# Linear attention into a gated FFN: the weight fold first, in column quarters over SyncE's queue, and the loads in a new order

## The chip, the cores and the metric

The kernel runs on one core of one Trainium2 chip. The metric is the device time of one execution in microseconds (us). A profiled execution gives the trace; its span runs from the first to the last instruction of the program.

## The reference

```python
def phi(x):
    return np.where(x > 0, x, np.exp(x) - 1.0) + 1.0
q_p, k_p = (phi(q), phi(k))                       # q, k, v: 8 batches, 8 heads, 576 tokens, 64
kv = np.einsum('bhsd,bhse->bhde', k_p, v)
z = np.sum(k_p, axis=2)
num = np.einsum('bhsd,bhde->bhse', q_p, kv)
den = np.einsum('bhsd,bhd->bhs', q_p, z)[..., None] + 1e-06
attn = num / den
...
x = attn.transpose(0, 2, 1, 3).reshape(4608, 512)
h = ((x @ w1) * (x @ w2)) @ w3                    # w1, w2: 512 x 1024; w3: 1024 x 1024
out = h @ w_out                                   # w_out: 1024 x 512
```

Inputs and output are f32 in HBM; the matmuls take bf16.

## The kernel before, in words

**The fold.** Since nothing stands between `@ w3` and `@ w_out`, the kernel multiplies the two weights once, `wf = w3 @ w_out`, and then needs one product per token block instead of two. For each of w3's eight row tiles (128 rows) `w3_tr` (L132) transposes eight 128x128 blocks on TensorE into a PSUM tile `w3p` and copies it to `w3t`; `wf_mm` (L139) then makes eight matmuls of 512 columns against `wo_sb` (w_out in bf16) and a copy into `wf_sb`.

**The work of a batch.** 512 of a batch's 576 tokens are handled per batch, as four blocks j of 128; the 64 that are left (the tail) are gathered over the batches into a ninth block, 8. For each batch, phi is made of k and q: an exp on ScalarE (`phi_exp`), a max and add on VectorE (`phi_max1`), a min on VectorE (`phi_min`), each for two halves g of four heads and for the tail. v is cast to bf16 (`v_unit`). `kv_full` multiplies k and v (L225, L229), `nat` (L262) multiplies q, transposed, with that (L280) and divides (L284 to L286) into `xn`. q is transposed either on TensorE (`q_tr`, L251, batches 0 and 1) or by a DMA (`qt_load`, L246); `xn` is transposed the same two ways (`xt_tr` L297, `xt_load` L304). The FFN of a block is eight F units (`f_unit`, L330: eight matmuls of 512 columns into `a_ps` and `b_ps`, a copy on ScalarE at L327, a product on VectorE at L328) and four O units (`o_unit` L475, eight matmuls of 512 columns each, and a copy), then stores (`o_store`); `o_last` (L497) does an O unit in two column halves, which are copied and stored by two engines.

**The order.** `ORDER` is a list written out in the program; each engine executes its own part of it in that order, and so does each DMA queue. A token is a letter, a batch and a part:

- loads: `M` q, `L` k, `N` v (512 KB a half), `R` the tails (part 0 four loads of 64 KB of q and k, part 1 two of v), `B` a column quarter of w1 (part 0) or w2 (part 1), `E` a w3 row tile, `C` w_out
- `x y z` exp, max and min of k, `X Y Z` of q, `v` the cast of v, `w` the transposes of a w3 tile, `u` a tile's fold matmuls
- `a` q's transposes on TensorE, `T` by DMA; `K` kv_full; `A` nat of block j; `P` xn's transposes on TensorE, `D` by DMA
- `F` and `O` the units (F0.7: unit 7 of block 0), `h` and `i` F0.0 and F0.1 step by step, `S H` stores, `Q` o_last, `I` constants

A "+" picks the other engine: for loads GpSimd's queue instead of SyncE's (SP), for copies VectorE instead of ScalarE.

**Queues.** The DMAs that SP issues and those that GpSimd issues each form one queue; both use the same 16 DMA engines. Only GpSimd's loads convert from f32 to bf16 on their way. So w3, w_out, w1 and w2 all go over GpSimd's queue and land as bf16. At the start SP issues half of q and k of batch 0 and its tails, and then nothing until the transposing DMAs at 45.6 us; all else of the front is GpSimd's, in the order q, w_out, w3, k, v, w3, k, w3, q of batch 1, k of batch 1, tails, w1 and w2 with v of batch 1 between them, tails. Each of the two queues has eight semaphores: a ninth load waits for the first one's landing. f32 loads of q, k and v go into the 13 buffers of the pool `ld`. `load_tail` (L99) issues four or two DMAs and returns the last.

**PSUM.** `mm_ps` has four banks (F units, fold), `o_ps_p` two (O units and transposes), `at_ps` one tile of two banks (kv_full and nat).

The functions for a Strassen scheme (`ws_make`, `xs_make`, `g_unit`, `s_make`, `w_unit`, `wt_make` and what they call) stand in the program, but the order has no token for them. `GATES` is empty.

## Time and profile before

| | us |
|---|---|
| median of 3 runs | 259.39 (259.12 to 259.40) |
| span of the profiled execution | 257.4 |
| around the span (median less span) | 2.0 |
| first matmul starts | 13.15 |
| first F unit starts | 40.70 |
| last matmul ends | 252.6 |
| TensorE busy | 232.3 (90%) |
| VectorE, ScalarE, GpSimd busy | 159.1, 116.8, 49.1 |
| HBM read, written | 38.80 MB, 9.44 MB |

The profiled execution is known by its span alone; what lies around it is taken from the runs' median. In the profile, PE is TensorE, PEld its weight loads, DVE VectorE, ACT ScalarE, POOL GpSimd and SP SyncE; L322 is line 322. Matmuls overlap, so a matmul's own duration (379 ns with 512 columns) is longer than its share of PE's time when matmuls follow each other (216 ns). A wait line names who waited, for whom, the total, how often, and the longest.

### The profile page before, as it was taken

The page shows a single profiled execution, that of the slowest core. Times are in us where ns is not written, and L with a number is a line of the kernel's source. Part 1 is how long each engine was busy: PE and PEld are TensorE (multiplying, and loading weights), DVE is VectorE, ACT ScalarE, POOL GpSimd, SP SyncE. Part 2 cuts the span into 40 slices and gives each one's busy share as a digit, 9 for nine tenths or more (in the row PEclk, how much of TensorE's full clock was granted, in tenths as well). Part 3 has the DMA queues.
Part 4 walks back from the last instruction along what each step waited for, and adds up shares of the span by engine and source line. Part 5 has one row for each costly group of instructions (what it writes and reads, how often), then busy time and mean ns, then how long its engine had stood idle before and what let it go on. Part 6 is the DMA issues. An engine that isn't in the chain of part 4 may idle for free.

```text
span 257.4 us, 3788 instructions
## 1 busy us (share of the span) xinstructions
PE 232.3 (90%) x1352; PEld 117.8 (46%) x1368; DVE 159.1 (62%) x350; ACT 116.8 (45%) x180; POOL 49.1 (19%) x84
## 2 busy tenths in 40 slices
PE   0087899999999869999999999999999999999992
PEld 0063565554454434445445445454544444444540
DVE  0548589778899426897887899978235633343200
ACT  1404677357756506755562473645332312332221
POOL 8524479455045100600000000000000000000000
PEclk9999999999999979999999999999999999999999
DMA  6999999999989999799999998646512143001124
GB/s 220 211 237 289 311 255 245 200 248 283 299 247 291 194 242 347 182 284 222 356 308 211 289 263 272 154 89 151 200 20 91 74 83 163 3 0 30 42 115 139
DMA packets 63762, 50.57 MB, mean 196 GB/s; under 512 B 33536, under 2 KB 58368, under 8 KB 63744
## 3 DMA queue, kind: packets, MB, share of 16 engines
q1 hardware_dynamic: 54432, 37.10, 55.9%
q0 software_dynamic: 9152, 13.11, 23.4%
q8 instruction: 10, 0.16, 0.3%
q10 hardware_dynamic: 160, 0.13, 0.2%
q14 instruction: 8, 0.07, 0.1%
HBM read 38.80 MB, written 9.44 MB: 187 GB/s over the span
## 4 chain that ended last, share of the span: by engine, by line
PE 78%; DMA 13%; DVE 4%; issue 2%; ACT 0%; POOL 0%; DVEq 0%; ACTq 0%; POOLq 0%
PE a_ps L322 24%; PE b_ps L322 23%; PE o_ps L479 21%; DMA v<-in_v_dram 5%; DMA qt<-qj 4%; PE nd L280 4%; DMA wt_sb<-in_moe_w_out_dram 4%; PE kvp L225 2%; PE wf_ps L143 1%; PE kvp L229 1%; DVE y L173 1%; DVE vt L204 1%; PE o_ps L504 1%; DVE kj L198 1%; DVE qj L198 0%
## 5 line engine op out<-in xcount | busy, mean ns | idle before, releaser
L322 PEld LDWEIGHTS <-w_sb 128*128 128x128 bf16 x576 | 55.3, 98 | 61.8 <-issue 0.9
L328 DVE TENSOR_TENSOR ab<-a_sb,b_ps 128x512 bf16<-128x512 f32 x72 | 49.1, 685 | 38.2 <-PE b_ps L322 30.5
L322 PE MATMUL a_ps<-xt,w_sb 128*128 128x512 bf16 x256 | 67.3, 382 | 0.0
L322 PE MATMUL b_ps<-xt,w_sb 128*128 128x512 bf16 x256 | 66.7, 379 | 0.0
L327 ACT COPY a_sb<-a_ps 128x512 f32<-128x512 f32 x72 | 41.8, 585 | 54.4 <-PE a_ps L322 48.9
L479 PE MATMUL o_ps<-wf_sb,ab 128*128 128x512 bf16 x267 | 63.7, 383 | 0.8 <-issue 0.2
L479 PEld LDWEIGHTS <-ab 128*128 128x128 bf16 x280 | 27.0, 98 | 30.2 <-issue 0.8
L481 ACT COPY o_sb<-o_ps 128x512 f32<-128x512 f32 x29 | 16.8, 585 | 43.4 <-PE o_ps L479 27.2
L286 DVE TENSOR_TENSOR xn<-nd,r 128x512 bf16<-128x512 f32 x32 | 22.1, 691 | 1.1
L168 ACT ACTIVATE e<-q 128x1024 bf16<-128x1024 f32 x16 | 16.7, 1056 | 8.5 <-DMA q<-in_q_dram 8.5
L168 ACT ACTIVATE e<-k 128x1024 bf16<-128x1024 f32 x16 | 16.6, 1056 | 5.2 <-DMA k<-in_k_dram 5.0
L280 PE MATMUL nd<-kv,qt 128*128 128x130 bf16 (+1 forms) x160 | 16.1, 223 | 2.6 <-DMA qt<-qj 2.1
L136 PE MATMUL w3p<-ident,w3b 128*128 128x128 bf16 x64 | 5.7, 242 | 13.7 <-DMA w3b<-in_moe_w_dram 13.7
L280 PEld LDWEIGHTS <-qt 128*128 128x128 bf16 (+1 forms) x160 | 11.6, 101 | 14.0 <-issue 3.3
L284 DVE TENSOR_SCALAR r<-nd 128x8 f32<-128x8 f32 (+1 forms) x40 | 6.5, 162 | 16.8 <-PE nd L280 16.4
L173 DVE TENSOR_SCALAR y<-q 128x1024 bf16<-128x1024 f32 x16 | 11.2, 707 | 8.7 <-DMA q<-in_q_dram 8.7
L143 PE MATMUL wf_ps<-wt_sb,w3t 128*128 128x512 bf16 x61 | 14.9, 380 | 0.7 <-DMA wt_sb<-in_moe_w_out_dram 0.5
L104 POOL DMA_DIRECT2D qk32r<-in_q_dram x14 | 9.0, 648 | 19.1 <-ACT a_sb L327 16.5
L198 DVE TENSOR_TENSOR qj<-e,y 128x512 bf16<-128x512 bf16 x32 | 11.9, 417 | 0.4 <-ACT e L168 0.3
L198 DVE TENSOR_TENSOR kj<-e,y 128x512 bf16<-128x512 bf16 x32 | 11.9, 418 | 0.2
L225 PE MATMUL kvp<-vt,kj 128*128 128x130 bf16 x128 | 9.8, 219 | 2.4 <-DVE vt L204 1.8
L136 PEld LDWEIGHTS <-w3b 128*128 128x128 bf16 x64 | 4.6, 109 | 15.0 <-DMA w3b<-in_moe_w_dram 14.5
(54 smaller groups left out, 180.3 us busy)
## 6 DMA issues: line engine op xcount, KB each, us to landing
out_dram<-o_sb SPq DMA_DIRECT2D x16, 512.0 KB, 3.7
q<-in_q_dram SPq DMA_DIRECT2D x13, 512.0 KB, 8.0
k<-in_k_dram SPq DMA_DIRECT2D x13, 512.0 KB, 6.7
v<-in_v_dram SPq DMA_DIRECT2D x12, 512.0 KB, 8.0
w3b<-in_moe_w_dram POOLq DMA_DIRECT2D x8, 256.0 KB, 12.0
v<-in_v_dram POOLq DMA_DIRECT2D x4, 512.0 KB, 9.8
w_sb<-in_moe_w_dram POOLq DMA_DIRECT2D x8, 256.0 KB, 6.9
q<-in_q_dram POOLq DMA_DIRECT2D x3, 512.0 KB, 11.2
```

The costliest lines, as they stand in the source:

```text
L143: nc.tensor.matmul(wfs[i], w3ts[i][:, kc, :], wo_sb[:, kc, :], start=(kc == 0), stop=(kc == FC - 1))
L168: nc.scalar.activation(out=e, in_=x, func=AF.Exp)
L173: (nc.gpsimd if alt else nc.vector).tensor_scalar(out=y, in0=x, scalar1=0.0, scalar2=1.0, op0=ALU.max, op1=ALU.add)
L198: nc.vector.tensor_tensor(out=p[0][:, 2 * g + c].rearrange("p j u d -> p u j d"), in0=e[:, c], in1=y[:, c], op=ALU.min)
L225: nc.tensor.matmul(kvp[:, i, g * W:(g + 1) * W], kj[:, hp, j].rearrange("p u d -> p (u d)"), vt[:, j, 2 * hp:2 * hp + 2, :].rearrange("p h ...
L280: nc.tensor.matmul(nd[rows, g, i * 2 * E1:(i + 1) * 2 * E1], w, kvs[b % 2][:, i, g].rearrange("p u e -> p (u e)"), start=True, stop=True)
L286: nc.vector.tensor_tensor(out=dst.rearrange("p (g h) e -> p g h e", g=2), in0=v4[:, :, :, 0:D], in1=r[rows].unsqueeze(3).to_broadcast([n, ...
L322: nc.tensor.matmul(ps, w[:, kc, f * P:(f + 1) * P], xt_of(c)[:, :, kc, :], start=(kc == 0), stop=(kc == KC - 1))
L327: nc.scalar.copy(out=a_sb, in_=a_ps)
L328: nc.vector.tensor_mul(out=abs_[c][:, f, :], in0=a_sb, in1=b_ps)
L479: nc.tensor.matmul(o_ps, ab[:, f, m * P:(m + 1) * P], wf_sb[:, f, :], start=(f == 0), stop=(f == FC - 1))
L481: copy_of(alt)(out=rows_of(c, m // 2)[:, m % 2], in_=o_ps)
```

## The change

- **The fold's first half comes first, by column quarters.** w3's row tiles 0 to 3 are loaded in four column quarters of 512 KB (`load_w3q`, token `c`; the first in two halves of 256 KB), w_out in four row quarters of 512 KB (`load_wo`, `C`), in turn, as f32 over SP's queue into the `ld` buffers. They are cast on chip: `w3_cast` (`g`, half a quarter each) and `wo_cast` (`G`). `q3_tr` (`W`) transposes a quarter's eight blocks, `q3_mm` (`U`) adds a quarter's two matmuls to a row tile's PSUM bank, so that four banks collect over the four quarters; `wf_copy` (`j`) is the copy. Row tiles 4 to 7 stay as they were (`E`, `w`, `u`), with the copy as a token of its own.
- **Loads.** All other loads of batches 0 to 2, w3's tiles 4 to 7, w1 and w2 go over GpSimd's queue, in one line: tails and k of batch 0, w3 and v in between, q, w3, then w1, w2 with k of batch 1, then v, tails and q of batch 1, then tails, k, v and q of batch 2. From batch 3 on all loads, tails too, go over SP's queue. Token `pC1` makes the next GpSimd load wait until w_out's second quarter is in; `qM1.1` makes the next SP load wait until q of batch 1 is in.
- **q of batch 0 by tokens.** Its halves are the blocks j 0, 1 and j 2, 3 of all heads, in runs of 512 B (`BY_TOKEN`), not four heads of all blocks in runs of 1 KB; `phi_min` and `q_tr` follow.
- **Tails of q in batches 0 and 1** are transposed on TensorE (two transposes, a0.2 and a1.2) instead of by DMA (T0.1, T1.1).
- **Twelve matmuls on zeros** (`zeros`, `d12`) at the start of TensorE's work.
- **Two F units of block 0 in token halves** (`f0.0.0` and so on), as the first two and the last two blocks j come; this takes the place of `h` and `i`.
- **nat** in batches 0 and 1 makes the last product in two halves; kvp and nd share one tile `at` that is allocated once.
- **The end.** Besides Q8.3, the last unit of all is an `o_last` (Q7.2), whose PSUM tile now comes from `mm_ps`.
- The order is a new one throughout. The Strassen functions and `GATES` go.

The diff's core:

```diff
+    def load_wo(qd):
+        t = raw["wo", qd] = ld.tile([P, HW], F32, tag="ld", name="wo32")
+        return nc.sync.dma_start(
+            out=t.rearrange("p (c n) -> p c n", n=DM),
+            in_=moe_w_out.rearrange("(c p) n -> p c n", p=P)[:, 2 * qd:2 * qd + 2, :])
+
+    def load_w3q(qd, h):
+        if ("w3q", qd) not in raw:
+            raw["w3q", qd] = ld.tile([P, HW], F32, tag="ld", name="w332")
+        ts = slice(2 * h, 2 * h + 2) if h < 2 else slice(0, 4)
+        return nc.sync.dma_start(
+            out=raw["w3q", qd].rearrange("p (t n) -> p t n", n=WQ)[:, ts],
+            in_=moe_w3.rearrange("(t p) n -> p t n", p=P)[:, ts, qd * WQ:(qd + 1) * WQ])
...
+    def w3_cast(qd, h, alt):
...
+        copy_of(alt)(out=raw["w3", 0][:, 2 * h:2 * h + 2, qd * WQ:(qd + 1) * WQ],
+                     in_=raw["w3q", qd].rearrange("p (t n) -> p t n", n=WQ)[:, 2 * h:2 * h + 2])
+
+    def wo_cast(qd, alt):
+        copy_of(alt)(out=wo_sb[:, 2 * qd:2 * qd + 2, :],
+                     in_=raw["wo", qd].rearrange("p (c n) -> p c n", n=DM))
+
+    def q3_tr(qd, alt):
+        t = w3ts["q", qd] = e_p.tile([P, 4, 2, P], BF16, tag="e", name="w3t", bufs=4)
+        tp = o_ps_p.tile([P, 4, 2, P], BF16, tag="ou"[qd % 2], name="w3p")
+        for i in range(4):
+            for c in range(2):
+                kc = 2 * qd + c
+                nc.tensor.transpose(tp[:, i, c, :], raw["w3", 0][:, i, kc * P:(kc + 1) * P], ident)
+        copy_of(alt)(out=t, in_=tp)
+
+    def q3_mm(qd, i):
+        if qd == 0:
+            wfs[i] = mm_ps.tile([P, DM], F32, tag="mm", name="wf_ps")
+        for c in range(2):
+            kc = 2 * qd + c
+            nc.tensor.matmul(wfs[i], w3ts["q", qd][:, i, c, :], wo_sb[:, kc, :],
+                             start=(kc == 0), stop=(kc == FC - 1))
...
+    def zeros(n):
+        for _ in range(n):
+            nc.tensor.matmul(at[:, 0], zero[:, 0:P], zero, start=True, stop=True)
...
+        js = slice(0, NJ) if half is None else slice(2 * half, 2 * half + 2)
+        for ps, w in ((a_ps, w1_sb), (b_ps, w2_sb)):
+            for kc in range(KC):
+                nc.tensor.matmul(ps[:, js.start * P:js.stop * P], w[:, kc, f * P:(f + 1) * P],
+                                 xt_of(c)[:, js, kc, :], start=(kc == 0 and half != 1),
+                                 stop=(kc == KC - 1), skip_group_check=half is not None)
...
-    M0.0+ Y0.0 C1 E0 M0.1 I0 X0.0 E3 X0.1 L0.0 Y0.1 Z0.0 Z0.1 C0 y0.0 w0+ R0.0 R0.1 x0.0 E4 x0.2
-    I1 w3+ L0.1+ x0.1 a0.0+ E1 y0.2 a0.1+ N0.1+ u0.2+ N0.0+ z0.0 R1.1 v0.1 y0.1 w4+ u3.2+ E2 w1+
...
+    I0 I3 c0.0 g0.0 d12 c0.1 g0.1+ I1+ C0 G0+ W0+ c1.2 g1.0 g1.1+ U0.3 W1 U0.2 U0.1 U0.0 C1 c2.2 G1
+    U1.1 U1.0 C2 g2.0 g2.1 U1.3 W2 U1.2 c3.2 g3.1+ G2 g3.0 W3 U2.0 C3 U2.3 pC1 R0.0+ R0.1+ G3+ y0.2
+    U2.2 U2.1 U3.0 L0.0+ U3.2 x0.2 x0.0 j2 E4 v0.2+ w4 U3.1 U3.3 y0.0 j0+ z0.2 u4.0 L0.1+ I2 y0.1
+    N0.0+ E5 u4.1 N0.1+ j3 x0.1 E6 M0.0+ M0.1+ j1 j4 a0.2 w5+ z0.0 u5.0 v0.0+ z0.1 E7 v0.1 u5.1 w6+
+    X0.0 B0.0 K0 Y0.0 Z0.0 Y0.1 u6.0 a0.0+ X0.1 w7 Z0.1 B0.1 A0.1 u6.1 a0.1 A0.0 u7.0 B1.0 B1.1 u7.1
+    P0.1 L1.0+ A0.3 j5 j7 P0.0+ A0.2 P0.3+ B2.0 B2.1 f0.0.0 A0.4 y1.0 j6 B3.0 B3.1 L1.1+ N1.0+ x1.0
+    P0.2 f0.1.0 f0.0.1 z1.0 f0.1.1 N1.1+ R1.0+ F0.2 y1.1 x1.1 R1.1+ z1.1 F0.7 v1.0 F0.4 M1.0+ y1.2
+    v1.1 x1.2 M1.1+ v1.2+ z1.2 F0.5 Y1.0 R2.0+ F0.3 R2.1+ X1.0 qM1.1 a1.2 L2.0+ Z1.0 Y1.1 X1.1 L2.1+
+    Z1.1 F0.6 a1.0 y2.2 K1 N2.0+ x2.2 a1.1+ N2.1+ v2.2 x2.0 M2.0+ O0.2 z2.2 y2.0 A1.2 M2.1+ z2.0
+    x2.1 R3.0 O0.3 A1.0 M3.1 v2.0 O0.0 y2.1 A1.3 v2.1 y3.2 z2.1 O0.1 P1.2 A1.1 P1.3 Y2.0 P1.0 R3.1
+    X2.0 M3.0 X2.1 P1.1+ Y2.1 x3.2 Z2.0 K2 Z2.1 Y3.1 R5.0 T2.0 L3.0 Y3.0 F1.7 F1.0 X3.1 N3.1 z3.2
+    A1.4 L3.1 Z3.1 X3.0 L4.0 F1.5 v3.2 F1.3 A2.2 F1.2 N3.0 x3.0 A2.3 x5.2 Z3.0 S0.1 y3.1 F1.1 A2.0
+    y3.0 x4.0 F1.4 R5.1 F1.6 x3.1 T3.0 A2.1 z3.0 z3.1 v3.0 y5.2 v3.1 D2.0 O1.1 y4.0 O1.0 K3 S0.0
...
+    S6.0 F7.3 H8.2 F7.5 Q8.3 O7.1 O7.0 S7.0 O8.1 O8.0 S8.0 O7.3+ H7.3 Q7.2
...
     def loaded(s, ins):
...
+        gate = "p" if ins.ins.engine == mybir.EngineType.Pool else "q"
+        if gate in held:
+            after(ins, held.pop(gate))
```

More of the change, by code (lines that the diff above doesn't have):

```diff
@@ L262, in nat @@
     def nat(b, j):
[L263 removed]
+        nd = at
         if j < NJ:
@@ L439, in snap @@
-    def snap(c, name, t):
-        s = snaps[c, name] = sm.tile([P, 2, HN], F32, tag="f", name=name, bufs=4)
-        nc.scalar.copy(out=s, in_=t)
+    o_sbs = {}
     def rows_of(c, r):
```

300 lines of the change are left out of this document (93 added, 207 removed).

## Prediction

> **What bounds the kernel now.** I read the page's 40 slices first, then the waits, then TensorE's timeline and the chain of waits, and then summed up stretches. The slices:
>
> ```profile
> PE   0087899999999869999999999999999999999992
> ...
> DVE  0548589778899426897887899978235633343200
> ...
> PEclk9999999999999979999999999999999999999999
> DMA  6999999999989999799999998646512143001124
> ```
>
> One slice is 6.4 us. PE is full from slice 5 on but for one dip (81 to 97 us), where the granted clock dips too. The DMA engines are nearly full from 6 to 170 us. The two waits of PE that matter:
>
> ```profile
> PE w3p L136 <- DMA w3b<-in_moe_w_dram: 13.7, 3, 13.1
> ...
> PE nd L280 <- DMA qt<-qj: 2.1, 1, 2.1
> ```
>
> PE stands 13.1 us until the first w3 row tile is there, and 2.1 us in the dip, for the transposed q of batch 3 (step A3.0).
>
> So I keep a ledger of TensorE. The chain of waits gives what one matmul takes behind another: 0.216 us with 512 columns (0.86 for four), 0.056 with 128 to 130 (0.45 for eight), 0.11 with 260. F units 576 x 0.216 = 124.6; O units 62.2; fold 64 x 0.216 = 13.8; transposes 128 x 0.056 = 7.2; nd 160 x 0.057 = 9.1; kvp 9.0. Together 225.9 us. PE's first matmul starts at 13.15 and its last ends at 252.6, so 13.6 us are lost in between. Where: A2.2 (first nd of batch 2) starts at 76.38; by the order, what stands before it (fold 17.4, F0 13.8, seven F1 12.1, two O0 3.5, K0 to K2 3.4, nd 2.3, transposes 3.6) is 56.1, so 7.1 are lost up to there. The dip costs 5.1:
>
> ```profile
> 40.60:76.40 35.80, 35.40 (x225) 18.14 (x224) 30.68 (x69) 20.48 (x34) 16.39 (x26) 1.00 1.18 249
> 85.80:92.20 6.40, 3.53 (x27) 1.92 (x26) 0.75 (x2) 3.02 (x6) 1.23 (x2) 1.00 1.25 147
> 92.20:97.00 4.80, 4.77 (x21) 2.23 (x22) 2.19 (x7) 0.00 (x0) 0.00 (x0) 0.64 1.17 274
> ```
>
> (Columns: PE, PEld, DVE, ACT, POOL busy, granted clock, DMA share, GB/s.) About 3.4 of them are waits in 85.8 to 92.2, 1.7 the clock at half for 3.4 us after it. 1.4 us are lost after 97. The transposition that is late, from the chain, and the start of the F units and the end, from the timeline:
>
> ```profile
> 81.07 11.12 DMA qt<-qj
> ```
> ```profile
> 40.70 1.03 PE L322 MATMUL a_ps<-xt,w_sb 128*128 128x512 bf16 x4
> ```
> ```profile
> 252.66 0.58 ACT L481 COPY o_sb<-o_ps 128x512 f32<-128x512 f32 x1 [1.10 <-PE o_ps L479]
> ```
>
> F0 starts at 40.7. After PE's end come that copy, two stores of one row block issued by SP one after the other, landing at 256.1, and the span's end at 257.4: a tail of 4.8 us. The runs' median is 259.39, 2.0 above this span; I work in the span and add 2.0.
>
> **The fold first.** Bytes do not change: 4 MB of w3, 2 MB of w_out, still read as f32. Half of w3 and all of w_out move to SP's queue. That queue's packets begin at 1.9 us; its first 512 KB land at 4.8, and alone it brings 512 KB in 1.4 to 1.5 us (two loads landing at 70.7 and 72.1). So c0.0 lands at 3.6, c0.1 4.8, C0 6.3, c1.2 7.8, C1 9.3, and alone C3 would land at 15.3. GpSimd's line is held until C1 is in, and behind that wait stand all its loads: batch 0, w1 and w2. Only the last of four tail loads carries it, three small ones go before it. Then 0.62 each for tails, 0.76 for a 512 KB load: L0.0 is issued at 11.2, and GpSimd's packets start 2.3 us after an issue (105.5 to 107.8): 13.5.
>
> From then the two queues share. Between 8 and 22 us the trace's packet records hold as many packets of one queue as of the other in every 2 us (309 and 310, 235 and 233, 309 and 311). GpSimd's take 0.16 to 0.19 us, SP's of 1 KB 0.047. About 20 of SP's packets per engine are left at 13.5; each waits for one of the others, +0.14: C3 lands at 18.3, k0.0 at 15.3, E4 at 16.9. After that GpSimd's line is alone at its own rate (between 27.6 and 35.3 five loads land, 1.55 each; w3 1.3; w1/w2 1.35): E5 21.3, v0 22.8, E6 24.1, E7 30, with 2.2 for each half of q0, whose runs are now 512 B. No row shows that form: by k/q rows it is 1.5; by tails, whose runs are 256 B, 0.17 to 0.6 per 64 KB, 1.4 to 5. I take 2.2, near the k/q rows. Then w1/w2 quarters at 31.4 to 42.4 with one k1 load among them, v1 46.9, q1 49.5 and 51.0, q2 last, 61, or 63.6 with SP's M3 loads beside it. (SP's own line is held from R3.0 on until M1.1 is in at 51; behind it stand M3 and T2.0, wanted later.)
>
> The casts: w3 halves 0.585 on ACT (five; row a_sb, 128x512) and about 0.42 on DVE (three; row xt on DVE, 128x512, 0.41), w_out 1.05 ACT and 0.73 DVE (vt rows), two each: ACT +5.0, DVE +2.7, before 20 us, where both stand waiting now (ACT 6.6, DVE 8.7). The twelve zero matmuls take 12 x 0.43 (the clock is half at first: eight transposes take 1.03 at 13.15, 0.61 later) from about 0.9 to 6.0, where PE has nothing to do.
>
> TensorE follows the landings: W0 6.0; U0 7.8 to 10.3; U1 done 13.4, U2 17.9, both behind ACT's casts; U3 at 19.1 (C3 and its cast); w4, u4 23.4; u5 26.4; K0 28.0; u6, a0; w7 30.5; u7 34.0; A0 and P0 35.5. F0 starts at 36, not 40.7.
>
> Then the loads lead. F0.7 needs B3.1 (42.4): it stands 1 us, F0 ends at 51. a1.0 and a1.1 need q1 (49.5, 51.0, plus 1.06 exp and 0.75 min, two halves): 1.4 us. O0, A1, P1, K2 and four F1 bring PE to 71.5. A2.2 needs T2.0: q2 at 63.6, its phi by 66.5, then 5.4 (68.6 to 74.0 in the trace) to 11.1: 72 to 77. I take **73.5**. Before A2.2 stand now 54.7 us of work (four O0 and four F1, not two and seven; +0.35 for the half F units and the tail transposes on PE). The old kernel was as far at 76.38 - 1.4 = 75.0. So the front is worth **-1.5**; all in time it is 70.2 (-4.8); with loads 4 us later 77.5 (+2.5), and 1.7 more if the clock falls.
>
> **The dip at A3.0.** T3.0 now stands ahead of A2.1, O1.1, O1.0, not behind. Its q3 is in by 68. On SP it is behind T2.0, five 512 KB loads, one store: 73.5 + 6 x 1.5 + 4.5 = 87. A3.0 is wanted at 73.5 + 6.9 + 0.7 + 3.5 + 1.1 + 1.7 = 87.4. It should just do: of 5.1 I let 1.6 stay: **-3.5** (0 to -5.1).
>
> **The end.** Q7.2 comes last: its second half is copied by ACT in 0.37 (row L506) and leaves by one store on ACT's queue, 2.0 to land: PE's end + 0.05 + 0.37 + 2.05 + 1.3 = 3.8 instead of 4.8: **-1.0**. SP's own stores are over by then (four of S8.0 end 1.9 us before PE does).
>
> **Small ones.** PE +0.4. The split xn multiply of batches 0 and 1: ten more DVE instructions of some 0.1, on an engine that is 86% busy from 41 to 76: 0 to +1. Tails on SP from batch 3 on: 30 issues of 0.65, beside idle SP time; if a waiting transpose holds them, 0 to +1. I take +0.2 for both. The deleted functions and GATES were never called by the order: nothing.
>
> Sum: -1.5 - 3.5 - 1.0 + 0.4 + 0.2 = -5.4: span 252.0, time **254.0**.
>
> **A page against the row.** A wait of 2.1 us, 0.6 and 0.3 before it, is followed by half clock here. The Trainium skill's "TensorE: Matmul & The Clock Gate" ("What's actually happening") lets the clock fall only after an idle window of about 3.4 us; by it a T2.0 wait of 2 us would cost 2 us, by the row 3.7.
>
> **Rivals.**
> (a) The front is bound by bytes: the same 21 MB stand before T2.0 (DMA share 1.1 to 1.2 in all that time), A2.2 gets no earlier than 75.0, and T3.0 is as late: only the end is won, 75.0 + 171.6 + 6.4 + 3.8 + 2.0 = 258.8. For it: the full DMA slices. Against: 52 to 72 us ran with 24 small tails between the loads at some 300 GB/s, which the new order spreads. The Trainium skill's "DMA: Bandwidth & Descriptors" ("Issuing engines are not separate DMA queues") says just this, that another issuing engine saves issue time alone; the alternating packets agree.
> (b) All lands in time: 70.2 + 171.6 + 1.4 + 3.8 + 2.0 = 249.0.
> (c) Slower: the fold's last quarters starve. If GpSimd's packets come before C2 and c3 are through, 96 packets an engine pair with slower ones, 0.2 each: C3 lands at 29.5, F0 starts at 45; 4.5 of these 9 us replace the later waits, and the clock falls once (1.7): 254.0 + 4.5 + 1.7 = 260.2. It decides from a C3 later than about 28.
> (d) Slower: one SP line. T3.0 after 93 us, behind loads that T2.0 held back, adds 4.4 and a second clock fall: 260.1.
>
> **Chances.** Forecast (251 to 257) 0.55, (a) 0.15, (b) 0.15, (c) 0.08, (d) 0.07. A measurement of this kernel tells about 0.2% (0.5 us); (a) lies on that border, half of it within. Faster 0.55 + 0.15 + 0.08 = 0.78, same 0.07, slower 0.15. For 8 in 10 I leave out the low half of (b) and most of (c) and (d): 249.5 to 259.4.
>
> **What would show it.** Right: first fold matmul near 8 us, C3 at 17 to 20, F0 at 35 to 37, short waits of PE for w_sb, q1 and qt, A2.2 at 72 to 75, no half clock near 90, one store last on ACT's queue. Wrong: F0 at 41 or later, a PE wait for qt over 2 us at batch 2 or 3, or a new half-clock stretch.

## The result, and the profile after

The changed kernel is slower: 270.13 us median (268.43 to 271.94) against 259.25 for the kernel before on the same chip. The ratio is 1.042, with an interval of 1.036 to 1.048. The forecast was 254.0. The profiled execution took 268.43 us with a span of 266.7, so 1.7 lie around it.

First the slices of the page of the changed kernel; one is now 6.7 us.

```profile
PE   8469888989699997999897999999999999999993
...
DVE  1315678779579956899593597786364443232301
...
PEclk9797999999889999999999999999999999999999
DMA  6999999889959988998999988982802014121025
```

TensorE starts at once, but the empty stretch of the old kernel (slices 1 and 2) has not gone. It has become holes: slices 2, 3 and 11, and more up to slice 22. The granted clock dips three times, and the DMA row, which before showed 9 from slice 2 to slice 11 and then an 8, has a 5 at slice 12.

The waits of TensorE tell whose those holes are (who waited, for whom: total, times, longest):

```profile
PE at L340 <- DVE xn L348: 4.6, 6, 1.7
PE wf_ps L174 <- DVE w3t L167: 3.9, 1, 3.9
PE xtp L363 <- ACT o_sb L412: 2.5, 2, 1.4
PE w3p L166 <- ACT w3b L153: 2.1, 1, 2.1
PE o_ps L410 <- DVE o_sb L412: 1.8, 1, 1.8
```

Before, TensorE waited directly for a DMA (13.7 and 2.1 us). Now it waits for VectorE and ScalarE. To see why, look at what those two engines stand at (further down).

The windows of the changed kernel (columns: PE, PEld, DVE, ACT, POOL busy, granted clock, DMA share, GB/s):

```profile
48.00:60.00 12.00, 10.68 (x74) 5.62 (x73) 8.89 (x20) 9.28 (x14) 8.88 (x13) 1.00 0.87 223
60.00:76.00 16.00, 13.08 (x87) 7.89 (x87) 12.42 (x35) 12.84 (x22) 1.86 (x3) 0.89 0.87 259
76.00:100.00 24.00, 24.00 (x145) 12.14 (x144) 18.85 (x46) 16.05 (x27) 0.00 (x0) 1.00 0.96 241
100.00:156.00 56.00, 50.45 (x286) 24.54 (x285) 41.09 (x94) 30.38 (x47) 0.00 (x0) 1.00 1.01 264
```

and of the kernel before:

```profile
48.00:60.00 12.00, 12.00 (x85) 6.13 (x83) 9.64 (x24) 5.35 (x10) 6.86 (x11) 1.00 1.21 239
60.00:76.00 16.00, 15.95 (x87) 7.80 (x87) 14.28 (x32) 10.80 (x18) 3.63 (x7) 1.00 1.08 272
76.00:100.00 24.00, 21.05 (x121) 10.31 (x122) 13.20 (x35) 11.03 (x18) 5.78 (x10) 0.93 1.15 263
100.00:156.00 56.00, 55.73 (x318) 27.57 (x320) 47.91 (x111) 32.47 (x49) 3.87 (x6) 1.00 1.02 264
```

Only 76 to 100 us has become better: the dip at A3.0 is gone. From 48 to 76 us TensorE lost what it had, with a DMA share of 0.87 instead of 1.1 to 1.2; from 100 to 156 it lost 5.3 us of busy time.

The ledger goes by starts: what passes from one matmul's start to the next beyond what the first takes when matmuls follow each other (0.216 us with 512 columns, as in the forecast; half clock counts as loss).

| | before | after |
|---|---|---|
| first matmul starts (without the twelve on zeros) | 13.15 | 6.29 |
| lost, 0 to 36 us | 5.8 | 12.3 |
| lost, 36 to 60 | 1.1 | 3.6 |
| lost, 60 to 76 | 0.2 | 5.2 |
| lost, 76 to 100 | 5.1 | 0.3 |
| lost, after 100 | 1.4 | 7.9 |
| first F unit | 40.70 | 41.19 |
| A2.2 (first nd of batch 2) | 76.4 | 82.5 |
| last matmul ends | 252.6 | 262.1 |
| span | 257.4 | 266.7 |

15.7 us more are lost, 6.9 of them merely because TensorE starts earlier. The first F unit, which the forecast put at 36, starts no sooner than before. From the timeline of TensorE in the changed kernel, that start and two holes behind it:

```profile
41.19 0.60 PE L389 MATMUL a_ps<-xt,w_sb 128*128 128x256 bf16 x4
...
59.16 0.73 PE L317 MATMUL tp<-ident,qj 128*128 128x128 bf16 x8 [1.21 <-DVE qj L246]
...
69.65 0.38 PE L363 MATMUL xtp<-ident,xn 128*128 128x128 bf16 x4 [1.42 <-ACT o_sb L412]
```

The first hole is a wait for phi of q of batch 1 (qj), whose load lands at 57.6 us (before: 35.3). In the second, TensorE waits for a copy of ScalarE, and ScalarE's timeline shows what that copy stood behind:

```profile
68.07 1.05 ACT L252 CAST vt<-v 128x1024 bf16<-128x1024 f32 x1 [1.78 <-DMA v<-in_v_dram]
69.02 0.58 ACT L412 COPY o_sb<-o_ps 128x512 f32<-128x512 f32 x1
```

The cast of v of batch 2 (vt) heads ScalarE's line, its load is late, and the copies that free TensorE's PSUM tiles stand behind it. After 100 us it is the same, with later batches:

```profile
103.08 0.43 DVE L215 TENSOR_SCALAR yr<-qk32r 128x512 bf16<-128x512 f32 x1 [1.37 <-DMA qk32r<-in_k_dram]
...
104.36 0.69 DVE L215 TENSOR_SCALAR y<-k 128x1024 bf16<-128x1024 f32 x1 [0.52 <-DMA k<-in_k_dram]
...
106.14 0.39 PE L340 MATMUL at<-kv,qt 128*128 128x130 bf16 x4 [1.71 <-DVE xn L348]
```

VectorE waits for a tail and a k of a later batch, and TensorE waits for the division (xn) behind them.

### The profile page after: what moved, and what is told of

Read it like the earlier page. It is cut to its first block, busy times and chain, and to the rows that moved or that the text cites. A ratio compares the mean times of both kernels' runs of the same rounds, so it can differ in the third digit from the quotient of the medians.

```text
span 266.7 us, 3914 instructions
## 1 busy us (share of the span) xinstructions
PE 242.0 (91%) x1408; PEld 122.9 (46%) x1408; DVE 158.0 (59%) x356; ACT 133.0 (50%) x205; POOL 36.7 (14%) x59
## 4 chain that ended last, share of the span: by engine, by line
PE 51%; DMA 30%; DVE 6%; SPq 4%; issue 3%; ACT 2%; POOL 1%; DVEq 0%; POOLq 0%; ACTq 0%
PE a_ps L389 17%; PE b_ps L389 17%; PE o_ps L410 12%; DMA k<-in_k_dram 9%; DMA v<-in_v_dram 8%; DMA w_sb<-in_moe_w_dram 4%; DMA wo<-in_moe_w_out_dram 4%; DMA w3b<-in_moe_w_dram 3%; PE at L340 2%; DMA q<-in_q_dram 2%; SPq L112 2%; DVE ab L396 2%; PE at L273 1%; PE o_ps L435 1%; DVE y L215 1%
## 5 line engine op out<-in xcount | busy, mean ns | idle before, releaser
L389 PE MATMUL b_ps<-xt,w_sb 128*128 128x512 bf16 (+1 forms) x264 | 66.0, 373 | 0.4 <-DVE ab L396 0.4
L389 PE MATMUL a_ps<-xt,w_sb 128*128 128x512 bf16 (+1 forms) x264 | 66.3, 373 | 0.0
L395 ACT COPY a_sb<-a_ps 128x512 f32<-128x512 f32 x72 | 41.9, 583 | 48.0 <-PE a_ps L389 40.6
L412 ACT COPY o_sb<-o_ps 128x512 f32<-128x512 f32 x28 | 16.4, 584 | 33.5 <-PE o_ps L410 27.3
L348 DVE TENSOR_TENSOR xn<-at,r 128x512 bf16<-128x512 f32 (+1 forms) x40 | 22.6, 582 | 1.1
L340 PE MATMUL at<-kv,qt 128*128 128x130 bf16 (+1 forms) x160 | 15.7, 220 | 5.0 <-DVE xn L348 4.6
L252 ACT CAST vt<-v 128x1024 bf16<-128x1024 f32 x12 | 12.5, 1049 | 6.8 <-DMA v<-in_v_dram 6.8
L174 PE MATMUL wf_ps<-wo_sb,w3t 128*128 128x512 bf16 x32 | 10.5, 475 | 4.2 <-DVE w3t L167 3.9
L215 DVE TENSOR_SCALAR y<-k 128x1024 bf16<-128x1024 f32 x16 | 11.5, 718 | 4.2 <-DMA k<-in_k_dram 4.1
L344 DVE TENSOR_SCALAR r<-at 128x8 f32<-128x8 f32 (+1 forms) x40 | 6.5, 161 | 11.3 <-PE at L340 10.8
L215 DVE TENSOR_SCALAR y<-q 128x1024 bf16<-128x1024 f32 x16 | 10.9, 687 | 1.4 <-DMA q<-in_q_dram 1.2
L412 DVE COPY o_sb<-o_ps 128x512 f32<-128x512 f32 x6 | 4.1, 688 | 11.1 <-PE o_ps L410 11.1
L273 PE MATMUL at<-vt,kj 128*128 128x130 bf16 x128 | 10.4, 231 | 0.0
## 6 DMA issues: line engine op xcount, KB each, us to landing
q<-in_q_dram POOLq DMA_DIRECT2D x6, 512.0 KB, 10.4
```

The lines of the kernel that those rows point to most:

```text
L215: (nc.gpsimd if alt else nc.vector).tensor_scalar(out=y, in0=x, scalar1=0.0, scalar2=1.0, op0=ALU.max, op1=ALU.add)
L252: copy_of(alt)(out=vt[:, :, 4 * i:4 * i + 4, 0:D], in_=raw["v", b, i].rearrange("p (h j d) -> p j h d", h=H // 2, j=NJ))
L273: nc.tensor.matmul(kvp[:, i, g * W:(g + 1) * W], kj[:, hp, j].rearrange("p u d -> p (u d)"), vt[:, j, 2 * hp:2 * hp + 2, :].rearrange("p h ...
L340: nc.tensor.matmul(nd[rows, g, i * 2 * E1:(i + 1) * 2 * E1], w, kvs[b % 2][:, i, g].rearrange("p u e -> p (u e)"), start=True, stop=True)
L348: nc.vector.tensor_tensor(out=x4[:, gs], in0=v4[:, gs, :, 0:D], in1=r[rows, gs].unsqueeze(3).to_broadcast([n, gs.stop - gs.start, 4, D]), ...
L389: nc.tensor.matmul(ps[:, js.start * P:js.stop * P], w[:, kc, f * P:(f + 1) * P], xt_of(c)[:, js, kc, :], start=(kc == 0 and half != 1), st ...
```

## The experiments

Eighteen kernels ran (there is no e17). Each ratio is to the kernel before on the same chip, with its interval. F0 is the start of the first F unit, A2.2 the first nd of batch 2. "Lost" is the ledger's sum over a stretch.

| run | median us | ratio | F0 | A2.2 | lost 36-76 | 76-100 | 100-156 |
|---|---|---|---|---|---|---|---|
| before | 259.25 | | 40.7 | 76.4 | 1.3 | 5.1 | 1.0 |
| changed kernel | 270.13 | 1.042 (1.036 to 1.048) | 41.2 | 82.5 | 8.8 | 0.3 | 7.1 |
| e1 | 270.12 | 1.041 (1.035 to 1.047) | 41.0 | 87.2 | 11.4 | 3.5 | 3.5 |
| e2 | 270.76 | 1.041 (1.034 to 1.047) | 40.9 | 81.9 | 8.7 | 0.9 | 7.2 |
| e3 | 270.80 | 1.046 (1.038 to 1.054) | 40.5 | 84.5 | 10.9 | 1.0 | 7.0 |
| e4 | 267.90 | 1.032 (1.027 to 1.038) | 41.2 | 84.7 | 10.4 | 2.4 | 2.7 |
| e6 | 269.44 | 1.037 (1.034 to 1.040) | 40.3 | 82.3 | 9.6 | 1.0 | 7.4 |
| e7 | 277.88 | 1.069 (1.065 to 1.073) | 54.6 | 89.7 | 4.7 | 1.4 | 7.9 |
| e8 | 273.22 | 1.052 (1.048 to 1.056) | 53.1 | 90.0 | 4.0 | 3.2 | 2.4 |
| e11 | 266.39 | 1.029 (1.022 to 1.035) | 40.3 | 82.9 | 8.7 | 2.5 | 2.7 |
| e12 | 272.04 | 1.048 (1.042 to 1.055) | 40.7 | 84.5 | 9.8 | 1.7 | 7.5 |
| e13 | 265.58 | 1.023 (1.017 to 1.028) | 40.8 | 78.9 | 6.1 | 0.1 | 7.2 |
| e14 | 263.60 | 1.016 (1.012 to 1.021) | 40.3 | 75.4 | 2.9 | 2.8 | 5.7 |
| e18 | 267.83 | 1.031 (1.026 to 1.037) | 41.7 | 80.5 | 6.4 | 1.1 | 8.1 |
| e19 | 264.58 | 1.022 (1.017 to 1.027) | 40.6 | 80.9 | 6.8 | 4.0 | 1.9 |
| e5 (on before) | 261.85 | 1.007 (1.004 to 1.010) | 40.4 | 75.9 | 1.1 | 0.1 | 7.3 |
| e10 (on before) | 257.39 | 0.993 (0.990 to 0.995) | 40.5 | 75.9 | 1.2 | 1.5 | 5.1 |
| e15 (on before) | 257.01 | 0.989 (0.985 to 0.993) | 40.3 | 75.8 | 1.2 | 3.0 | 1.7 |
| e16 (on before) | 259.77 | 1.000 (0.997 to 1.003) | 40.4 | 76.4 | 1.6 | 6.0 | 1.4 |

### Three mends of single places, and all together (e1 to e4)

The first theory was that three local waits make the loss, each to be mended by itself. In e1 the tails of batches 3 to 7 go back to GpSimd's line:

```diff
-... R3.0 ... R3.1 ... R7.1 ...
+... R3.0+ ... R3.1+ ... R7.1+ ...
```

> The changed kernel, but the tail loads of batches 3 to 7 go over GpSimd's queue again (30 loads of 64 KB; all else as changed). Theory L (late loads: with tails, halves, stores and transposes in SP's one line, loads come late, and VectorE and ScalarE stand at the head of their line for them, which costs TensorE the 7 to 8 us that are lost after 100 us): 4 to 7 us faster than the changed kernel's 270.1, so 263 to 266, and the waits of TensorE for xn and o_sb between 100 and 156 us gone. Theory F (the front alone sets the time, what is late afterwards is a consequence of a late q2 and k2): no change, 268 to 272.

In e2 the loads of q of batch 1 come ahead of that batch's tails, and the tails of batch 2 go over SyncE's line:

```diff
-... R1.0+ R1.1+ M1.0+ M1.1+ ... R2.0+ R2.1+ ...
+... M1.0+ M1.1+ R1.0+ R1.1+ ... qN1.1 R2.0 R2.1 ...
```

> The changed kernel, but in the front q of batch 1 goes ahead of batch 1's tails in GpSimd's line, and batch 2's tails go over SP's queue, held until v of batch 1 is in. Theory S (a queue holds eight loads; six small tails take six of the eight places, so from 48 to 60 us the DMA engines, 0.87 busy instead of 1.2, have too little to do): q of batch 1 lands at 54 to 55 instead of 57.6, q of batch 2 at 68 to 70 instead of 73.3, the time falls by 2 to 4 us to 266 to 268. Rival B (the front is bound by bytes, the order within it moves nothing): q of batch 2 stays at 73, 268 to 272.

In e3 the gate on GpSimd's line sits on the first of the four tail loads, not on the last:

```diff
-                ins = (nc.gpsimd if alt else nc.sync).dma_start(
+                last = (nc.gpsimd if alt else nc.sync).dma_start(
...
+                ins = ins or last
```

> The changed kernel, but the wait for w_out's second quarter stands at the first of the four tail loads of batch 0, not at the last, so that no load of GpSimd's queue runs beside the first loads of the fold. Theory T (the three small loads that run ahead hold up one of the 16 DMA engines, so that w_out's first quarter lands at 9.8 instead of 6.3 and all behind it late): w_out's first quarter at 6.3 to 7, first fold matmul near 8 instead of 11.2, the gate opens at 9.5 to 10 instead of 12.6, F0 starts 2 to 3 us earlier than 41.2, the time falls by 2 to 3 us. Rival: SP's queue alone is that slow (loads of 2 KB pieces), w_out stays at 9.8 and the time at 268 to 272.

> The three edits together (late tails on GpSimd's queue, front tails aside, all tails of batch 0 behind the gate). If theories L, S and T each hold and add up: 8 to 12 us faster than the changed kernel, 258 to 262, level with the kernel before. If the front alone sets the time: the gain of the two front edits, 263 to 266. If none holds: 268 to 272.

Each mend did what it was meant to do at its own place: in e1 the loss after 100 us fell from 7.1 to 3.5, in e2 q of batch 1 landed at 55.1 instead of 57.6, in e3 the first fold matmul ran at 8.5 instead of 11.2. None of the three moved the time clear of the intervals; the three together brought it to 267.9, which lies between two of the expected ranges. What took the place of the old wait is visible in e1, on VectorE:

```profile
74.07 0.43 DVE L215 TENSOR_SCALAR yr<-qk32r 128x512 bf16<-128x512 f32 x1 [5.71 <-DMA qk32r<-in_k_dram]
```

The order has batch 3's tail early in VectorE's line, because SyncE's line brings it early. On GpSimd's line it came at 74, and VectorE stood 5.7 us for it. And e3 showed a second thing: the fold was 3 us earlier, but F0 only 0.7.

### The late tails, from both sides (e5, e11)

e5 makes the suspected cause on the kernel before, which has no other part of the change:

```diff
-... R3.0+ ... R7.1+ ...
+... R3.0 ... R7.1 ...
```

> The kernel before with one edit: the small tail loads of batches 3 to 7 go out on SyncE's line, as the change has them, instead of GpSimd's; all else is as before. Theory 'one line for the late loads' (SyncE's line with stores, transposes, big loads and thirty tail issues of 0.65 us each runs late after 100 us): the loss of TensorE between 100 and 156 us rises from 1.0 to 3 to 5 us, time 261.5 to 264. Rival 'only the late front matters' (the losses after 100 us in the changed kernel come from batches that were already late at 76 us): 259.0 to 260.3.

The loss between 100 and 156 us rose from 1.0 to 7.3, and the time to 261.85, at the lower end of what the theory gave, although the loss was more than the 3 to 5 us expected, because the dip at A3.0 had gone as well, which the expectation had not seen: with the tails of batches 3 to 5 off GpSimd's line, the loads and the transpose for A3.0 are sooner (T3.0 lands at 87.3, before at 92.2). Nearly all of the new loss is one wait, on TensorE and then on VectorE (timelines of e5):

```profile
140.14 0.59 PE L280 MATMUL nd<-kv,qt 128*128 128x130 bf16 x4 [5.17 <-DVE kv L234]
```

```profile
138.19 0.43 DVE L173 TENSOR_SCALAR yr<-qk32r 128x512 bf16<-128x512 f32 x1 [6.50 <-DMA qk32r<-in_k_dram]
```

TensorE waits for a copy (kv of batch 5) that stands in VectorE's line behind the tail of batch 7. That tail is not needed for a long time. But on SyncE's line its four issues stand behind the transposing DMA of batch 5, which took from 125.2 to 133.4 to issue.

e11 takes back, in the changed kernel, only the tails of batches 4 to 7:

```diff
-... R4.1 ... R4.0 ... R5.0 ... R7.1 ...
+... R4.1+ ... R4.0+ ... R5.0+ ... R7.1+ ...
```

> The changed kernel with the tails of batches 4 to 7 back on GpSimd's line, those of batch 3 left on SyncE's (with all five back, run e1, VectorE stood 5.7 us at 68 for batch 3's tail, which came late on GpSimd's line, and nothing was won). Theory: the loss between 100 and 156 us falls from 7.1 to 2 to 4 and nothing comes in its place, 265 to 267. Rival 'the next late load': 268.5 to 271.

266.39 us: the loss between 100 and 156 us fell from 7.1 to 2.7. So the late line costs about 3.7 us in the changed kernel (the two intervals, 1.022 to 1.035 and 1.036 to 1.048, do not meet). e11 shows it by taking the tails away, and e5 makes the same kind of loss on the kernel before.

### Two lines for the front, and no gate (e6, e7, e8)

e6 gives the six big loads of batch 1 to SyncE's queue, behind E7:

```diff
-... L1.0+ ... L1.1+ N1.0+ ... N1.1+ ... M1.0+ ... M1.1+ ...
+... qE7 L1.0 ... L1.1 N1.0 ... N1.1 ... M1.0 ... M1.1 ...
```

> The changed kernel with the six 512 KB loads of batch 1 on SyncE's queue, held until E7 (the last w3 row tile, 33.8 us in the changed kernel) is in, instead of on GpSimd's line behind w1 and w2. Theory 'one front line' (after 36 us GpSimd's line alone, with eight places and 24 small loads in it, starves the DMA engines: share 0.87 from 48 to 76 us against 1.1 to 1.2 before): the share in that stretch rises above 1.0, q1 lands by 48, first nd of batch 2 by 78 instead of 82.5, time 264 to 267. Rival 'order of bytes' (what counts is how many MB stand ahead of q2, 21.4 against 19.9 before): q1 earlier, but q2 and the first nd of batch 2 within 1.5 us of 82.5, time 268.5 to 271.

The rival was right: A2.2 at 82.3, q of batch 2 in at 72.6 instead of 73.3. The share from 48 to 60 us rose to 1.02, but what SyncE's queue brought was taken from w1 and w2, whose last quarter came at 52.8 instead of 46.2. TensorE then stood for that, and the clock was at half for 6.8 us from 48.8 on.

e7 takes `pC1` out of the order, and e8 joins e6, e7 and e1.

> The changed kernel without the gate on GpSimd's line: its loads of batch 0 start at once, beside the fold's quarters on SyncE's queue, instead of after C1 is in. Theory 'bytes in front' (one queue alone brings some 250 GB/s in its first 6 us, two bring more; F0 waits for the 10 MB ahead of it and for what follows the last of them, whichever comes first): 5.3 MB or more have landed by 20 us instead of 4.6, first fold matmul later (13 to 15), first F unit at 39 to 41, time 267 to 270. Rival 'fold first is what helps' (the gate keeps the fold's loads quick, its early matmuls are worth something): C3 at 25 or later, first F unit at 43 to 45, time 272 to 275.

> The changed kernel with three edits: no gate on GpSimd's line, batch 1's loads on SyncE's queue behind E7, and the tails of batches 3 to 7 back on GpSimd's line. If all three causes are right (bytes in front, one front line, one late line) they are worth their sum: some 2 + 4 + 3 off 270, that is 259 to 263. If a batch that is late at one place only hands its wait to the next (as the three earlier mends did), 266 to 269.

e7 ended in the rival's way and beyond it: C3 lands at 33.4, F0 starts at 54.6, 277.88 us. The bytes landed by 20 us were the same 4.59 MB; only their order differed. So the gate is worth nearly 8 us to the changed kernel. e8 took 273.22 us, above both of its expected ranges and 4.7 less than e7. e7 is the forecast's rival (c) made real, and the price is higher than it said: F0 was put at 45 for a C3 at 29.5.

### What a load costs by itself (e9)

> No attention and no FFN: this kernel only loads, in eight groups, each held until the group before is in, and stores zeros-like sums; its time says nothing beside the others. Groups 1 to 6 hold four loads of 512 KB f32 source each: w3 column quarters on SyncE's queue; w_out on SyncE's; w3 rows cast to bf16 on GpSimd's; k on GpSimd's, not cast; v on SyncE's; q by token (512 B runs) on SyncE's. Group 7: four w3 quarters on SyncE's beside four k on GpSimd's; group 8: four v on SyncE's beside four cast w3 rows on GpSimd's. Theory 'form': the cast rows bring source bytes 15 to 25% faster than quarters or w_out (1.2 to 1.3 us per load behind another, against 1.45 to 1.6), by-token q takes 1.5 to 2.2, and two queues together bring no more than one (2.9 to 3.1 us per pair in group 7, under 2.8 in group 8). Rival 'queue': every load takes 1.45 to 1.55 whatever its form, and two queues together are faster than one (under 2.6 per pair in both).

The groups were not held apart: GpSimd's loads ran beside SyncE's from the start, so groups 3 and 4 and the pairs can't be read as planned. Where one queue ran alone, loads landed behind each other by 1.50 us (w3 quarters: 48.47, 49.98, 51.48, the first of them 1.50 behind another load), 1.50 (v: 32.88, 34.38, 35.88) and 1.80 (q by token: 41.58, 43.39, 45.18, 46.97, the first 1.80 behind another load). With both queues at work, 17 loads of 512 KB of different forms landed between 7.57 and 30.52 us, 1.35 each. So by-token q costs 1.80, not the 2.2 of the forecast, and two queues bring about a tenth more than one. Whether a load that is cast on its way is quicker stays open: no stretch has cast rows alone (two of them and one v landed within 3.90 us, 1.30 each).

### The order inside batch 2 (e12)

```diff
-... L2.0+ L2.1+ N2.0+ N2.1+ M2.0+ M2.1+ ... K2 Z2.1 ... T2.0 ... F1.3 A2.2
+... M2.0+ M2.1+ N2.0+ N2.1+ L2.0+ L2.1+ ... Z2.1 T2.0 ... z2.1 ... K2 F1.3 A2.2
```

(X2, Y2 and Z2 change places with x2, y2 and z2 as well.)

> The changed kernel with batch 2's q loaded and worked on before its k, T2.0 right behind it, and K2 three F units later. In the changed kernel q2 is the last of batch 2 (73.3 us), the transpose T2.0 starts behind it and takes 4.7 more; before, q2 came first (63.7), k2 and v2 landed beside the transpose. Theory 'order inside batch 2': T2.0 lands at 74 to 77 instead of 80.5, first nd of batch 2 at 77 to 79.5 instead of 82.5, time 265.5 to 268. Rival 'bytes': K2 now waits for k2 as A2.2 did for q2, first nd of batch 2 at 81 to 83, time 269 to 271.

T2.0 landed at 74.1 instead of 80.5, and A2.2 came at 84.5 all the same. In neither kernel did TensorE wait for that transpose: in the changed one it landed 2.0 us ahead of A2.2. TensorE was late by itself, with 6.1 us lost between 60 and 76, behind ScalarE's casts as in the changed kernel. A transpose 6 us earlier bought nothing: 272.04 us, above both expected ranges.

### Fewer bytes, fewer small loads (e13, e14)

e13 leaves out E4 to E7 and takes the transposes of row tiles 4 to 7 from the first four:

```diff
-            loaded(s, load_w3(b))
+            pass
...
-            nc.tensor.transpose(tp[:, kc, :], raw["w3", 1][:, i % 4, kc * P:(kc + 1) * P], ident)
+            nc.tensor.transpose(tp[:, kc, :], raw["w3", 0][:, i % 4, kc * P:(kc + 1) * P], ident)
```

> The changed kernel without the loads E4 to E7 (2 MB of w3, row tiles 4 to 7); their work is done on the first four row tiles again, so the lower half of the folded weight is that of the upper half. It shows what 2 MB fewer ahead of batches 1 and 2 are worth. Theory 'bytes': at 1.5 us per 512 KB everything on GpSimd's line comes 6 us earlier (q0 at 25 to 27, q1 at 51 to 52), first F unit at 35 to 37, first nd of batch 2 at 76 to 78 instead of 82.5, time 262 to 265. Rival 'places': q1 and v2 still come as late, behind the tails, first nd of batch 2 at 80 to 83, time 267 to 270.

e14 leaves out the tail loads of batches 1 and 2:

```diff
+            if b in (1, 2):
+                raw[("qk", "v")[i] + "r", b] = raw[("qk", "v")[i] + "r", 0]
+            else:
+                loaded(s, load_tail(b, i, alt))
```

> The changed kernel without the twelve 64 KB tail loads of batches 1 and 2; their tail rows are taken from batch 0's. It shows what these small loads on GpSimd's line cost. Theory 'places' (each holds one of eight places for 4 to 7 us; the DMA engines fall to a share of 0.87 from 48 to 76 us while q1 waits to be issued): share above 1.0 in that stretch, q1 at 52 to 54, v2 at 63 to 65, first nd of batch 2 at 77 to 79, time 263 to 266. Rival 'bytes' (they are 0.8 MB, 2 us): first nd of batch 2 at 80 to 82, time 267 to 270.

e13 bears most on F0. It took 265.58 us with A2.2 at 78.9, between its two expectations. Two MB that had stood ahead of everything were gone, q of batch 0 landed 3.5 us sooner, and the timeline of e13 still has

```profile
40.34 0.39 PE L340 MATMUL at<-kv,qt 128*128 128x130 bf16 x4 [1.06 <-DVE xn L348]
40.57 0.38 PE L363 MATMUL xtp<-ident,xn 128*128 128x128 bf16 x4
40.79 0.60 PE L389 MATMUL a_ps<-xt,w_sb 128*128 128x256 bf16 x4
```

So F0 is not held by those loads alone. From the landing of C3 to F0 it is 21.8 us in the changed kernel, 21.1 in e13 and 21.2 in e7, though C3 lands at 19.35, 19.7 and 33.4. In that stretch TensorE has 15 to 16 us of work. The rest is some 4 to 5 us of waits for one copy after another and, in the changed kernel and e7, some 2 us more because the clock is at half for 3.4 and 4.1 us of it. The copies come by turns with the work: the w3 transposes go to a PSUM tile, ScalarE copies it in 1.01 us, the matmuls follow, and phi of k, q and the casts of v are in the same two lines. Where C3 is early, E7 takes over: it lands at 33.5 to 34.9 in the changed kernel, e3, e11, e14, e18 and e19, and F0 follows 6.6 to 7.4 later in all six (e3, with C3 as early as 16.3, had F0 at 40.5). So two limits end together near 41, and moving the loads alone (e3, e13) did next to nothing. That the copies make the first limit is read from the timelines; no run shortened them.

e14 is the run that moves the front most: A2.2 at 75.4, earlier than theory 'places' had it, and 263.60 us, in the theory's range. Its window:

```profile
48.00:60.00 12.00, 12.00 (x86) 6.68 (x85) 10.46 (x24) 11.16 (x19) 1.80 (x3) 1.00 1.03 344
```

344 GB/s instead of 223, and TensorE full. The twelve small loads land only 0.2 us behind each other (51.61, 51.81, 52.02 and so on in the changed kernel), so themselves they take some 2.6 us. But v of batch 2, which stands behind them, came at 57.5 and 59.1 instead of 68.1 and 69.7. A good part of the rest of those 10.5 us is that GpSimd's line ran empty: q of batch 1 was issued at 50.1 and 51.9 as places came free, and landed 4.2 and 5.6 us after. In e14 it was issued at 40.8 and 42.0. The first of the two issues, in the changed kernel and in e14:

```profile
50.09 0.76 POOL L103 DMA_DIRECT2D q<-in_q_dram  x1 [1.07 <-DMA v<-in_v_dram]
```

```profile
40.79 0.75 POOL L103 DMA_DIRECT2D q<-in_q_dram  x1 [0.62 <-DVE r L345]
```

A second thing stands beside it in the changed kernel. From 58 us on SyncE's line brings q and the tails of batch 3, released by q of batch 1, and the two queues take turns (63 to 69 us: 496 packets of GpSimd's, 490 of SyncE's). In that time k and v of batch 2 landed 3.3 to 3.9 us behind each other (60.9, 64.7, 68.1). What this costs was not tried by itself.

### The twelve tails on another line, and the two mends that held (e18, e19)

```diff
-... R1.0+ ... R1.1+ ... R2.0+ ... R2.1+ ...
+... E7 qE7 R1.0 R1.1 R2.0 R2.1 ...
```

> The changed kernel with the twelve tail loads of batches 1 and 2 on SyncE's line, which is idle from 19 to 51 us, behind E7 (33.8 us); nothing is left out. Theory 'places' (their cost is that they hold GpSimd's eight places while q1 and batch 2 wait to be issued): nearly as in e14, w_sb's last quarter about 1 to 2 us later than 46.2, q1 at 52 to 54.5, v2 at 60 to 63, first nd of batch 2 at 75 to 78, time 263 to 266. Rival 'the loads as such': beside w1 and w2 they take as much from the DMA engines as on GpSimd's line, first nd of batch 2 at 80 to 83, time 267.5 to 271.

> The changed kernel with the tails of batches 1 and 2 on SyncE's idle line behind E7 (as e18) and those of batches 4 to 7 on GpSimd's (as e11). If the two mends add up (6.5 by e14, 3.7 by e11): 259 to 262, the loss against before is accounted for. If the second gives back part of the first (loads that come earlier find their in-order readers waiting for the next one): 262 to 265.

e18 came out as the rival had it: A2.2 at 80.5, 267.83 us, both at the lower end of its ranges. Beside GpSimd's queue the tails are not cheap either. In the trace's packet records the DMA engines take from the two queues by turns: from 40 to 46 us 1450 packets of GpSimd's and 1446 of SyncE's, from 46 to 52 us 802 and 800, from 52 to 58 us 518 and 516. SyncE's are 256 bytes long (0.02 to 0.03 us), GpSimd's up to 4 KB (0.16 to 0.2). So a tail of 64 KB, 256 small packets, landed 6 to 20 us after its issue and held a place for that time; w1 and w2 ended at 50.8 instead of 46.2, q of batch 1 at 59.1. In return batch 2's v came at 65.2 instead of 69.7.

The Trainium skill, "DMA: Bandwidth & Descriptors" ("Queues, rings and completion order"), has the DMA engines go round the queues packet by packet; the counts agree. With equal counts, SyncE's queue of small packets got few bytes here beside GpSimd's large ones.

e19 took 264.58 us. The two mends gave 2.3 (e18) and 3.7 (e11), and together 5.6: within the intervals (some 1.5 us each) they add up. The time lies in the second expected range, 262 to 265, not because one mend gave back part of the other but because e18's part was smaller than the 6.5 counted for it.

### The end alone (e16)

```diff
-... Q8.3 O7.0 O7.1 O7.2 S7.0 O7.3 O8.0 S7.1 O8.1 S8.0
+... Q8.3 O7.1 O7.0 S7.0 O8.1 O8.0 S8.0 O7.3+ H7.3 Q7.2
```

> The kernel before with only the last nine steps of its order exchanged for those of the change: batch 7's last rows come last, in two column halves, with one store on each of two queues. By the forecast the end from TensorE's last matmul falls from 4.8 to 3.8 us: 258.0 to 258.8. Rival (the changed kernel's own end took 4.6 us, its last stores 2.9 us to land instead of 2.0, because stores go out on two queues at once): 259.0 to 259.8.

No difference: 1.000 (0.997 to 1.003). From TensorE's last matmul to the end it is 4.9 us in e16, 4.6 in the changed kernel, 4.8 before. The last two stores of the changed kernel, from its timeline:

```profile
262.16 0.37 ACT L437 COPY o_sb<-o_ps 128x256 f32<-128x256 f32 x1 [2.93 <-PE o_ps L435]
262.37 0.39 SPq L440 DMA_DIRECT2D out_dram<-o_sb  x1
262.56 0.35 ACTq L440 DMA_DIRECT2D out_dram<-o_sb  x1
```

The copy and the single store are as short as forecast. But seven stores are issued within 3.7 us, the last one lands 2.9 us after its issue, the first of them 2.3 (in the old kernel the last one took 2.3), and what was won ahead of it is gone.

### A version that is faster than both (e10, e15)

What e5 and e11 say together is that some tails are better on SyncE's line and some are not. So on the kernel before, e10 moves the tails of batches 3 to 6 and e15 those of 3 to 5:

```diff
-... R3.0+ ... R5.1+ ...
+... R3.0 ... R5.1 ...
```

> The kernel before with the tails of batches 3 to 6 on SyncE's line, those of batch 7 left on GpSimd's. Theory: with all five on SyncE's (run e5) the dip at A3.0 was gone, but VectorE stood until 138.1 us for batch 7's tail, queued behind the transpose of batch 5 on SyncE, and TensorE lost 5.3 us to it; with that tail on GpSimd's line both losses are gone, 254 to 257, faster than before. Rival: the wait moves to the next load that is late on SyncE's line, 258 to 262.

> The kernel before with the tails of batches 3 to 5 on SyncE's line, batches 6 and 7 left on GpSimd's. Run e10 (3 to 6) lost 5.1 us between 100 and 156, against 1.0 before. If batch 6's tail on SyncE's line is part of that (its transposes of batches 4 and 5 come later behind it), 254 to 256.5; if the losses there come from TensorE being 3 us earlier than the loads, whatever their line, 256.5 to 258.5.

257.39 us, ratio 0.993 (0.990 to 0.995), and 257.01, 0.989 (0.985 to 0.993). Both are faster than the kernel before, by 0.7 and 1.1%; between the two the intervals do not decide. e10 fell between its two expected ranges and e15 in its second one. The windows of e15, beside those of before above:

```profile
76.00:100.00 24.00, 21.43 (x135) 10.84 (x133) 15.39 (x39) 12.48 (x20) 1.22 (x2) 1.00 1.13 264
100.00:156.00 56.00, 55.23 (x314) 26.90 (x313) 46.86 (x107) 31.35 (x48) 4.00 (x6) 1.00 1.06 278
```

In e15 the dip is smaller (3.0 us lost instead of 5.1), the clock stays full, and after 100 us little is given back. In e10 the expected end of both losses did not come: its dip shrank to 1.5, but 5.1 were lost after 100, the longest waits being 1.2, 0.8 and 0.7 us.

## Why the prediction was wrong, point by point

Two steps of the prediction failed: the front, from "F0 starts at 36" to A2.2 at 73.5, and the term "Tails on SP". The forecast's terms came to -5.4 us in the span. Measured by the same places, the span grew by 9.3:

| term | forecast | measured |
|---|---|---|
| front: A2.2 against "as far" at 75.0 | -1.5 | +7.5 (82.5) |
| dip at A3.0 | -3.5 | -4.8 (5.1 lost before, 0.3 after) |
| after 100 us ("DVE, SP") | +0.2 | +6.5 (7.9 lost against 1.4) |
| the end | -1.0 | -0.2 |
| more work on TensorE | +0.4 | +0.4 (by count, not measured apart) |

They sum to +9.4, 0.1 from the 9.3.

- **The fold first.** The steps up to U3 held, though later: C3 at 19.35 (18.3 forecast), U3's transposes at 19.6 (19.1). But "first fold matmul near 8" was 11.2. The term that was too small is the start: three tails that the gate doesn't hold (7.4, 8.5 and 9.9 us) ran beside the first quarters, C0 came at 9.8 instead of 6.3, C1 at 12.6 instead of 9.3, and with it the gate opened 3 us late. In e3, where they are held too, C0 came at 7.0 and C1 at 9.9.
- **"F0 starts at 36."** This step failed outright. The forecast walked from landing to landing ("w4, u4 23.4; u5 26.4; K0 28.0") and took ScalarE and VectorE as free to copy at once: from C3 to F0 it had 17.7 us, where TensorE's work alone is 15 to 16. The runs show two limits in its place: some 21 us of transposes, copies and matmuls by turns behind C3 (e7, e13), and E7, 3.8 us later than forecast, with 6.6 to 7.4 us behind it. F0 came at 41.2; "F0 at 41 or later" had been named as the sign of a wrong forecast.
- **"q1 49.5 and 51.0, q2 63.6."** They came at 54.3 and 57.6, and at 73.3. The step had counted landings at 1.5 us each as though GpSimd's line were always full. It was not: from 48 to 76 us the DMA share was 0.87, because twelve tails and the loads behind them shared eight places (e14, against e13 with more bytes gone and less won). A clock at half for 3.4 us, from 71.9 on, followed the holes at 68 to 71 us.
- **A2.2 at 72 to 77** was 82.5. It was not the late T2.0 that set it (e12), but TensorE's own holes from 57 to 72 us.
- **The dip at A3.0** came out nearly in size: no wait for qt, no half clock near 90. But that is in part luck. T3.0 landed at 94.6, 7.6 later than forecast, and cost nothing only because A3.0 was 9.3 late itself (96.7 instead of 87.4). In e14, with the front in time, A3.0 came at 89.6, 0.5 after T3.0, and 2.8 us were lost from 76 to 100. On the old kernel the tails alone bring the gain in full (e5) or in part (e15).
- **"Tails on SP ... 0 to +1."** The mechanism was named ("if a waiting transpose holds them") and the size was far off: the loss after 100 us grew by 6.5, and of the 7.1 lost up to 156 us e11 takes back 4.4 by moving four batches' tails. What was missed is who waits: a tail's max heads VectorE's line, and the copies for TensorE stand behind it. One such wait cost 5.2 us in e5. Rival (d) had this line as its cause, at T3.0; it decided elsewhere.
- **The end** was right in its copy (0.37) and its one store on ACT's queue. But SyncE's stores were not "over by then": the last of them was issued at 262.4, after TensorE's end. And the last store took 2.9 us to land, not 2.0.
- **The rivals.** Rival (a), that the front is bound by bytes, had F0's true reason in part: bytes moved forward push others back. By 20 us 4.59 MB of source had landed against 5.64 before, by 60 us 18.15 against 19.14. So the missing megabyte was lost before 20 us; from 20 to 60 us both kernels brought some 13.5 MB. Rival (a) gave 258.8 because it let A2.2 come at 75.0. The "some 300 GB/s" that it was weighed against, for 52 to 72 us, are 267 in the trace. Rival (c) did not happen, thanks to the gate, as e7 shows.

Against the page on the clock: the forecast weighed a fall after waits of some 2 us (its row) against an idle window of about 3.4 (the Trainium skill, "TensorE: Matmul & The Clock Gate", "What's actually happening"). In the changed kernel the clock fell three times. The holes there were 4.1 us (7.0 to 11.2), 2.3 (17.3 to 19.6), and two of 1.6 and 1.2 with little work between. Each fall lasted 3.4 us. So the row held again: two of the three falls came with holes shorter than the page's window. The traces show a closer rule. The granted clock changes in steps of 3.41 us, and in the step before each fall TensorE was busy, counted as in the ledger, for 0.02, 0.32 and 0.21 of it (0.33 in the kernel before); the least busy step at full clock with no fall behind it had 0.50 (0.46). Over the two kernels and the seventeen variants of them, the 33 steps before a fall have 0.37 at most, and the 1306 others 0.36 at least.

What stays open: e19 gets back 5.6 of 10.9 us without leaving work out. The other half lies in the front, as A2.2 at 80.9 in e19 against 75.0 shows. The twelve tails (6.5, e14) and the late tails (3.7, e11) would account for 10.2 if they added up, but the two were not run together, and e14 leaves work out. That it is the place of batch 1's loads behind w1 and w2 (they landed by 43 us before, by 57.6 after) is argued from the landings and was not tried by itself; e6, which tried the queue and not the order, doesn't decide it.
